# A DRAIN of its own on GpSimd, ahead of the last expert's four scatters

## The chip, the cores and the metric

The kernel runs on one core of one Trainium2 chip. The core has five engines that follow their own instruction queues: TensorE (PE), VectorE (DVE), ScalarE (ACT), GpSimd (POOL) and SyncE (SP); 16 DMA engines move data beside them. The metric is the device time of one execution in microseconds; lower is better. Three executions of the kernel before took 489.33, 487.57 and 484.19 us, median 487.57 us.

## What is computed

Banded attention with eight global columns, whose output rows are the tokens of a mixture-of-experts layer: 3072 tokens of 512 values, 8 experts, top 1, at most 768 tokens per expert. The reference, cut to its core:

```python
x = attention(q, k, v)                       # 4 x 8 heads x 768 x 64 -> (3072, 512)
expert_idx = np.argmax(x @ w_gate, axis=1)
gate_w = softmax(x @ w_gate)[np.arange(N), expert_idx]
# disp[e]: the rows of x that go to expert e, in order, up to the capacity
h = np.maximum(np.einsum('ecd,edf->ecf', disp, w1), 0.0)
y = np.einsum('ecf,efd->ecd', h, w2)
out[i] = gate_w[i] * y[expert_idx[i], pos[i]]     # for each token that was kept
```

## The kernel before

The program has three stages. The first is attention with the gate's logits and the routing: it leaves the rows of x in a DRAM tensor (`xrows`), and each token's expert and place in tables on the chip. The second is a loop over the eight experts (e = 0 to 7), each with four blocks of up to 128 tokens. The third, `overflow`, is skipped by one branch (L1279) where no expert has more than four blocks, as in the profiled execution.

For one expert GpSimd first fetches the four blocks of rows by indirect DMAs (`fetch_rows`, L519: 128 rows of `xrows`, named by a column of indices). TensorE turns them, multiplies by w1 in eight steps (`layer1`, L548) and by w2 (`layer2`, L1122 to L1124, and `beside`, L1135, for a few rows of the last block), with every factor split in a high and a low part. At the end of an expert `last()` (L1245) closes the four output blocks: `finish` (L1022) scales a block by the tokens' gates on ScalarE into the tile `ysb` (L1024; the fourth block has three additions on VectorE, L1028), and the `scatter` that it returns (L1031) has GpSimd send the 128 rows of `ysb` to their tokens' rows of the output by an indirect DMA (L1032). `out_scatters` lists all scatters so far; `apart` tells the scheduler that they write different rows. `last()` of expert e runs inside the first step of expert e + 1, and for e = 7 behind the loop (L1259).

GpSimd issues no other DMAs. Over the whole program it issues 32 gathers (L519) and 32 scatters (L1032), four of each per expert.

PE, ACT and DVE follow the order in which the code is written. GpSimd's queue in this stage is ordered by Tile's scheduler. In the built program GpSimd's queue around the last expert reads: the seventh expert's four scatters, six branches, the last expert's four scatters, a register load from `nblk` (L1237), the branch over `overflow` (L1279), two semaphore instructions, and the closing sequence, which has the line of the launch (L1367): DRAIN, barrier with the other four engines, DRAIN, a clearing of the semaphores, DRAIN, second barrier. A scatter's instruction waits for the block in `ysb`, and for the DMA that used the same one of eight semaphores before. SP waits at the end until every DMA has landed, then joins the barrier.

Of the kernel before, what the change touches and what calls it, by code (L numbers as in the profile page):

```python
# [120 lines left out]
def fused(ctx: ExitStack, tc, q, k, v, wg, w1, w2, out, dims, n_global, n_local, cap):  # L121
    nc = tc.nc
    B, H, S, D = dims
    DM, E = wg.shape
# [41 lines left out]
    NOSYNC = mybir.DependencyInfo(mybir.DependencyClass.NoSync, mybir.DependencyReason.SCHED_ONLY)  # L166
# [294 lines left out]
    def apart(w, others):  # L461
        for o in others:
            tc.declare_no_dep(w.ins, o.ins, reason="each token has a row of its own")
        others.append(w)
# [17 lines left out]
    def token_rows(t, e, lo, hi):  # L482

        ids, gates = filled.rearrange("p c (e a) -> p c e a", a=RB)[:, :, e, lo:hi].rearrange("p c e a -> c p e a")
        nc.vector.tensor_scalar(t.bitcast(I32)[:, :, :, 0], ids, float(N), None, op0=ALU.add)
        nc.vector.tensor_copy(t[:, :, :, 1], gates)
# [54 lines left out]
    def layer1(e, f, h_ps, xh, xl, s, parts=(0, 1)):  # L541
        w = wparts[e * (NF // FP) + f // FP][0]
        w1h, w1l = w["h"], w["l"]
        fs = slice(f % FP * P, (f % FP + 1) * P)
        for part in parts:
            n = 2 * KC * part
            for c, (ww, xx) in ((c, t) for c in range(KC) for t in (((w1h, xh), (w1l, xh)), ((w1h, xl),))[part]):
                nc.tensor.matmul(h_ps[:, s], ww[:, c, fs], xx[:, c, s], start=n == 0, stop=n == 3 * KC - 1)  # L548
                n += 1
# [451 lines left out]
    def gather(gi, rows=(), xhl=None):  # L1001

        xh, xl = xhl or [moe.tile([P, KC, T4], F32R, name=n) for n in ("xh", "xl")]
        rows = list(rows)

        def fetch():
            for a in range(len(rows), FIXED):
                xg, ld = fetch_rows(moe, "xg", FIXED + 1, gi(a))
                rows.append(xg)
            return ld  # L1010

        def turn(a, ps=None):
            ps = bankC([P, KC, P]) if ps is None else ps.rearrange("p (c t) -> p c t", c=KC)
            turn_rows(ps, rows[a])
            o = slice(a * P, (a + 1) * P)
            nc.scalar.copy(xh[:, :, o], ps)
            nc.vector.tensor_tensor(xl[:, :, o], ps, xh.bitcast(F32)[:, :, o], op=ALU.subtract)
        return xh, xl, turn, fetch

    out_scatters = []  # L1020

    def finish(e, a, rows, y):  # L1022
        ysb = moe.tile([P, DM], F32, name="ysb", bufs=FIXED)
        nc.scalar.activation(ysb, y, AF.Copy, scale=rows[:, 1:2])  # L1024
        if a == FIXED - 1:

            for n, o, m in ((1, 2 * GR, 2 * GR), (0, GR, GR), (0, 3 * GR, GR)):
                nc.vector.scalar_tensor_tensor(ysb[0:m], y[o:o + m], gates[0:m, e, n:n + 1], ysb[0:m],  # L1028
                                               op0=ALU.mult, op1=ALU.add)

        def scatter():  # L1031
            w = nc.gpsimd.indirect_dma_start(  # L1032
                out=out, out_offset=bass.IndirectOffsetOnAxis(ap=rows.bitcast(U32)[:, 0:1], axis=0),
                in_=ysb, in_offset=None, bounds_check=N - 1, oob_is_err=False)
            apart(w, out_scatters)
        return scatter


# [57 lines left out]
    def load_arm(e):  # L1096
        arms[e] = nc.values_load(arm[0:1, e:e + 1], engines=[PE], min_val=0, max_val=NV - 1)
# [6 lines left out]
    def widths(e):  # L1104

        def among(lo, hi):
            if hi - lo == 1:
                yield FINE * (lo + FIRST_ARM)
                return
            mid = (lo + hi) // 2  # L1110
            with tc.If(arms[e] > mid - 1) as more:
                yield from among(mid, hi)
            with more.Else():
                yield from among(lo, mid)
        yield from among(0, NV)

    def layer2(e, f, a, y, hh, hl):
        w = wparts[e * (NF // FP) + f // FP][1]
        w2h, w2l = w["h"], w["l"]
        t = slice(a * P, (a + 1) * P)  # L1120
        fi = f % FP
        nc.tensor.matmul(y, hh[:, t], w2h[:, fi], start=f == 0, stop=False)  # L1122
        nc.tensor.matmul(y, hh[:, t], w2l[:, fi], start=False, stop=False)  # L1123
        nc.tensor.matmul(y, hl[:, t], w2h[:, fi], start=False, stop=f == NF - 1)  # L1124

    def beside(e, fs, w, hs):

        y = y_ps[FIXED - 1]
        a, rows = w // P, -(-(w % P) // GR) * GR
        if rows in (GR, 2 * GR):  # L1130
            n = P // rows
            for f in fs:
                o = f % n * rows
                hr = hs[f][2]
                nc.tensor.matmul(y[o:o + rows], hr[:, (a - SURE) * P:(a - SURE) * P + rows],  # L1135
                                 wparts[e * (NF // FP) + f // FP][1]["r"][:, f % FP], start=f < n, stop=f >= NF - n)

    def whole(w):

        return range(SURE, w // P + (w % P > 2 * GR))  # L1140
# [7 lines left out]
    def fetch(step, after=()):  # L1148
        if step < STEPS and step not in wparts:
            pieces[step] = raw_weights(step, moe, "wr", 4, after, plain)  # L1150
# [40 lines left out]
    for e in range(E):  # L1191
        xh, xl = xs[0:2]
        hs = hs0 if e == 0 else {}

        def second(fs, a, e=e, hs=hs):
            for f in fs:
                layer2(e, f, a, y_ps[a], *hs[f][0:2])

        for f in range(NF):
            step = (e * NF + f) // FP  # L1200
            if f % FP == 0:
                fetch(step + SPLIT + 1)
                split = pieces.pop(step + SPLIT, [])
            if f == 1 and 0 < e < E - 1:
                xs = gather(lambda a, e=e: gi[:, e + 1, a:a + 1])
                xs[3]()
            if f == 2 and e == 0:
                load_arm(0)
            if f == 4 and e + 1 < E:
                load_arm(e + 1)  # L1210
            h = h_ps[f % 2]

            fs = (f - 2,) if f > 1 else ()
            for a in range(SURE):
                second([i for i in fs if e > 0 or i >= EARLY], a)
            part = slice(FIRST * P if e == 0 and f < EARLY else 0, T4)
            for w in widths(e) if e > 0 or f > 1 else ():
                for a in whole(w):
                    second(fs, a)
                if f == 5:  # L1220
                    beside(e, range(0, 4), w, hs)
                layer1(e, f, h, xh, xl, slice(part.start, w))
            if f == 3 and e == 0:
                tb = moe.tile([P, E, FIXED, 2], F32, name="tb", bufs=1)
                token_rows(tb, slice(0, E), 0, FIXED)
                nc.vector.tensor_scalar(gi, tb.bitcast(I32)[:, :, :, 0], N - 1, None, op0=ALU.min)
                xs = gather(lambda a, e=e: gi[:, e + 1, a:a + 1])
                xs[3]()
            hidden(hs, f, part)
            if f == 0 and last is not None:  # L1230
                last()
            if f == 3 and e == 0:
                to = take_beside(tb)
            if f == 5 and e == 1:
                count_blocks()
            if f == 4 and e == E - 1:
                most = nc.values_load(nblk[:, E:E + 1], min_val=0, max_val=max(RB, FIXED + 1))  # L1237
            for piece in () if f == 0 else split if f == 1 else split[2 * (f % FP):2 * (f % FP) + 2]:
                piece()

            turned = {5: (0, 1), 6: (2, 3)} if e == 0 else {3: (0,), 4: (1,), 5: (2,), 6: (3,)}
            for a in turned.get(f, ()) if e + 1 < E else ():
                xs[2](a)

        def last(e=e, second=second, hs=hs):  # L1245
            for a in range(SURE):
                second((NF - 2,), a)
            for w in widths(e):
                beside(e, range(4, NF), w, hs)
                for a in whole(w):  # L1250
                    second((NF - 2, NF - 1), a)
            rest = [finish(e, a, to[:, e, a - SURE], y_ps[a]) for a in range(SURE, FIXED)]
            rest[0]()
            for a in range(SURE):
                second((NF - 1,), a)
                finish(e, a, first["early"][:, a] if e == 0 and a < FIRST else tb[:, e, a], y_ps[a])()
            rest[1]()

    last()  # L1259
    manual[0].__exit__(None, None, None)  # L1260

# [109 lines left out]
```

## Time and profile before

| | |
|---|---|
| three executions | 489.33, 487.57, 484.19 us; median 487.57 us |
| the profiled execution, its own time | 488.32 us |
| its span, first to last instruction | 486.5 us |
| granted TensorE clock, mean | 0.969 of full speed |
| TensorE, matmuls | 452.5 us busy (93%) |
| VectorE, ScalarE | 287.4 us (59%), 282.5 us (58%) |
| GpSimd | 157.9 us (32%), 353 instructions |

Times in the profile are counted from the span's first instruction. Each engine has a sequencer, and rows of its instructions end in q (POOLq, SPq): DRAIN, semaphore and branch instructions are such rows. They are not counted as busy, and the chain of work that ended last, which the page follows back from the end, does not hold them all; it is followed from the last instruction that is counted as work. So what an engine does between its last work and the end of the span has to be asked for by line.

### The profile page before, as it was taken

To read this page: it belongs to the slowest core of one execution; us is meant where nothing else is said; L and a number is where in the kernel's file an instruction comes from. 1 tells how busy PE (TensorE), PEld (TensorE's weight loads), DVE (VectorE), ACT (ScalarE), POOL (GpSimd) and SP (SyncE) were. 2 spreads that over 40 slices of the span, in tenths; PEclk is the share of its full clock that TensorE was granted. 3 is DMA by queue.
4 is the path that set the end of the run, shared out by engine and by line. 5 is a ranking of instruction groups with operands and counts; after the bars stand their busy time and mean duration, and the time that the engine had idled before them with its cause. 6 is when DMAs were issued, how large, how long until landed. Compare 5 with 4: busy or idle time off the path is not lost.

```text
span 486.5 us, 11872 instructions
## 1 busy us (share of the span) xinstructions
PE 452.5 (93%) x4147; PEld 372.9 (77%) x4147; DVE 287.4 (59%) x935; ACT 282.5 (58%) x786; POOL 157.9 (32%) x353
## 2 busy tenths in 40 slices
PE   7999999989987699999999999999999999999690
PEld 3777877776776587888889989889889888887570
DVE  6687888778776626445646546456556455545421
ACT  5999898979862124445455555546556455446330
POOL 7117537789981104312103213103203203003002
PEclk9999999999996699999999999999999999999995
DMA  7988777787412078646536636446545545142001
GB/s 228 272 269 260 233 243 225 253 275 214 150 60 68 23 262 303 197 131 201 175 88 222 190 122 205 140 136 199 179 132 198 150 137 202 51 130 72 5 5 51
DMA packets 58701, 80.94 MB, mean 166 GB/s; under 512 B 6125, under 2 KB 34797, under 8 KB 58576
## 3 DMA queue, kind: packets, MB, share of 16 engines
q1 hardware_dynamic: 52912, 64.44, 42.0%
q0 software_dynamic: 5120, 14.69, 9.1%
q8 instruction: 94, 1.54, 1.3%
q14 instruction: 31, 0.25, 0.2%
q10 hardware_dynamic: 544, 0.02, 0.1%
HBM read 66.54 MB, written 14.68 MB: 167 GB/s over the span
## 4 chain that ended last, share of the span: by engine, by line
PE 51%; issue 28%; POOL 14%; DVE 3%; ACT 2%; POOLq 0%; DVEq 0%; ACTq 0%
PE bankC L548 17%; PE y L1122 5%; PE y L1124 5%; PE y L1123 5%; PE pair L689 3%; POOL put L449 3%; PE pair L723 3%; PE bankC L749 3%; PE bankC L752 3%; POOL out_dram L1032 2%; POOL own_row L444 2%; POOL xg L519 1%; PE bankC L500 1%; POOL w2l L267 1%; ACT sc L700 1%
## 5 line engine op out<-in xcount | busy, mean ns | idle before, releaser
L548 PE MATMUL bankC<-xh,w1h 128*128 128x416 f32 (+5 forms) x268 | 91.2, 345 | 2.6 <-issue 1.4
L1161 ACT ACTIVATE hh<-bankC 128x512 fp32r<-128x512 f32 (+1 forms) x67 | 38.7, 579 | 94.1 <-PE bankC L548 94.1
L548 PE MATMUL bankC<-xh,w1l 128*128 128x416 f32 (+5 forms) x268 | 89.8, 340 | 1.2 <-issue 1.2
L1162 DVE SCALAR_TENSOR_TENSOR hl<-bankC,hh 128x512 fp32r<-128x512 f32 (+1 forms) x67 | 44.6, 667 | 74.0 <-ACT hh L1161 73.6
L700 ACT ACTIVATE sc<-sc,mx 128x168 f32<-128x168 f32 (+1 forms) x192 | 80.3, 422 | 4.3 <-DVE mx L664 4.2
L1122 PE MATMUL y<-w2h,hh 128*128 128x512 f32 x192 | 79.8, 416 | 0.9 <-ACT hh L1161 0.8
L1124 PE MATMUL y<-w2h,hl 128*128 128x512 f32 x192 | 76.4, 398 | 0.0
L1123 PE MATMUL y<-w2l,hh 128*128 128x512 f32 x192 | 76.2, 397 | 0.0
L519 POOL DMA_INDIRECT xg<-xrows,gi x28 | 28.5, 1018 | 117.7 <-PE bankC L500 99.6
L548 PEld LDWEIGHTS bankC<-xh,w1h 128*128 128x128 f32 x268 | 51.6, 193 | 10.6 <-issue 6.0
L548 PE MATMUL bankC<-xl,w1h 128*128 128x416 f32 (+5 forms) x268 | 58.7, 341 | 0.6 <-issue 0.6
L664 DVE CUSTOM_DVE_ANT_0 sc<-pair,bias 128x168 f32<-128x168 f32 (+1 forms) x192 | 53.0, 317 | 9.7 <-PE pair L689 8.3
L1032 POOL DMA_INDIRECT out_dram<-ysb,to x16 | 15.9, 994 | 126.0 <-ACT ysb L1024 123.6
L548 PEld LDWEIGHTS bankC<-xh,w1l 128*128 128x128 f32 x268 | 51.7, 193 | 4.0 <-issue 1.3
L275 DVE TENSOR_TENSOR w1l<-wr,w1h 128x512 fp32r<-128x512 f32 x58 | 37.5, 689 | 27.8 <-ACT w1h L272 27.8
L1164 ACT ACTIVATE hr<-bankC 128x256 f32<-128x256 f32 x64 | 24.6, 385 | 49.3 <-DVE hl L1162 49.3
L275 DVE TENSOR_TENSOR w2l<-w2r,w2h 128x512 fp32r<-128x512 f32 x58 | 37.5, 688 | 19.2 <-ACT w2h L272 17.3
L548 PEld LDWEIGHTS bankC<-xl,w1h 128*128 128x128 f32 x268 | 47.9, 192 | 1.1 <-issue 0.4
L1122 PEld LDWEIGHTS y<-w2h,hh 128*128 128x128 f32 x192 | 36.6, 190 | 12.5 <-issue 4.6
L1124 PEld LDWEIGHTS y<-w2h,hl 128*128 128x128 f32 x192 | 36.4, 189 | 8.9
L1123 PEld LDWEIGHTS y<-w2l,hh 128*128 128x128 f32 x192 | 36.6, 191 | 6.1
L689 PE MATMUL pair<-K,q 64*64 64x168 f32 (+1 forms) x768 | 36.9, 309 | 1.3 <-DMA q<-in_q_dram 1.1
(190 smaller groups left out, 768.8 us busy)
## 6 DMA issues: line engine op xcount, KB each, us to landing
wr<-in_moe_w_dram SPq DMA_DIRECT2D x58, 256.0 KB
w2r<-in_moe_w_dram SPq DMA_DIRECT2D x58, 256.0 KB
K<-in_k_dram SPq DMA_DIRECT2D x24, 256.0 KB
q<-in_q_dram SPq DMA_DIRECT2D x24, 256.0 KB
v<-in_v_dram SPq DMA_DIRECT2D x24, 256.0 KB
xrows<-xr SPq DMA_DIRECT2D x23, 256.0 KB
v<-in_v_dram SPq DMA_DIRECT2D x20, 192.0 KB
wst<-in_moe_w_dram SPq DMA_DIRECT2D x12, 256.0 KB
```

The lines of the kernel that those rows point to most:

```text
L275: (nc.gpsimd if meanwhile else nc.vector).tensor_tensor(parts["l"][:, s], r, parts["h"].bitcast(F32)[:, s], op=ALU.subtract)
L519: ld = nc.gpsimd.indirect_dma_start(out=xg, out_offset=None, in_=xrows[0:n], in_offset=bass.IndirectOffsetOnAxis(ap=gi.bitcast(U32), axis= ...
L548: nc.tensor.matmul(h_ps[:, s], ww[:, c, fs], xx[:, c, s], start=n == 0, stop=n == 3 * KC - 1)
L664: x = nc.vector.tensor_tensor_reduce(out=un["sc"][:, a, 0:un["w"]], in0=un["ps"][hh][:, gg, :], in1=un["bias"][:, 4 * (u % 2) + a, :], sca ...
L689: made = nc.tensor.matmul(pss[hh][r * HP:(r + 1) * HP, gg, :], st_[i]["q"][rows, g, q0:q0 + HP], kq[rows, g, k0:k0 + w], start=True, stop= ...
L700: nc.scalar.activation(sc[:, a, 0:w], sc[:, a, 0:w], AF.Exp, bias=un["mx"][:, a:a + 1], scale=-1.0, accum_out=st_[i]["sm"][:, 4 * half + a ...
L1032: w = nc.gpsimd.indirect_dma_start(out=out, out_offset=bass.IndirectOffsetOnAxis(ap=rows.bitcast(U32)[:, 0:1], axis=0), in_=ysb, in_offset ...
L1122: nc.tensor.matmul(y, hh[:, t], w2h[:, fi], start=f == 0, stop=False)
L1123: nc.tensor.matmul(y, hh[:, t], w2l[:, fi], start=False, stop=False)
L1124: nc.tensor.matmul(y, hl[:, t], w2h[:, fi], start=False, stop=f == NF - 1)
L1161: nc.scalar.activation(hh[:, s], h[:, s], AF.Relu)
L1162: nc.vector.scalar_tensor_tensor(hl[:, s], h[:, s], 0.0, hh.bitcast(F32)[:, s], op0=ALU.max, op1=ALU.subtract)
```

## The change

One instruction is added to GpSimd's queue. In `last()` of the last expert (e = E - 1) `nc.gpsimd.drain()` is made, ordered behind every scatter made so far, that is those of experts 0 to 6, and ahead of the first scatter of the last expert. The orderings are of the kind NOSYNC: they fix places in GpSimd's own queue and add no semaphore. `scatter` returns its instruction, so that `last()` can name it. The whole diff:

```diff
@@ -1033,6 +1033,7 @@
                 out=out, out_offset=bass.IndirectOffsetOnAxis(ap=rows.bitcast(U32)[:, 0:1], axis=0),
                 in_=ysb, in_offset=None, bounds_check=N - 1, oob_is_err=False)
             apart(w, out_scatters)
+            return w
         return scatter
 
 
@@ -1250,7 +1251,13 @@
                 for a in whole(w):
                     second((NF - 2, NF - 1), a)
             rest = [finish(e, a, to[:, e, a - SURE], y_ps[a]) for a in range(SURE, FIXED)]
-            rest[0]()
+            if e == E - 1:
+                done = nc.gpsimd.drain()
+                for w in out_scatters:
+                    tc.add_manual_dep(done.ins, w.ins.name, NOSYNC)
+            w = rest[0]()
+            if e == E - 1:
+                tc.add_manual_dep(w.ins, done.ins.name, NOSYNC)
             for a in range(SURE):
                 second((NF - 1,), a)
                 finish(e, a, first["early"][:, a] if e == 0 and a < FIRST else tb[:, e, a], y_ps[a])()
```

In the built program the new DRAIN stands directly behind the seventh expert's fourth scatter, ahead of the six branches. It waits for no semaphore and sets none. Every other instruction of the five queues stands in the same order as before, with the same waits. Line numbers from 1036 on are one higher in the changed file and from 1253 on seven higher, so the DRAIN is at L1255 and the closing sequence has L1374.

## Rows read from the trace of the kernel before

**Rows 1.** Page, part 1: busy time, share of the span, instructions of each engine.

```profile
PE 452.5 (93%) x4147; PEld 372.9 (77%) x4147; DVE 287.4 (59%) x935; ACT 282.5 (58%) x786; POOL 157.9 (32%) x353
```

**Rows 2.** Chain that ended last, its last two pieces: start, length, what.

```profile
448.26 24.97 issue
...
477.31 0.98 POOL out_dram L1032
```

**Rows 3.** Closing line L1367, whole span: engine, operation, count, ns min/median/max, first to last start.

```profile
L1367 POOLq DRAIN  x3: 40/107/5306, 480.3 to 486.2; - x3
L1367 SPq DRAIN  x3: 7/7/13, 480.5 to 485.9; - x3
L1367 PEldq DRAIN  x2: 8/8/8, 475.4 to 486.0; - x2
L1367 ACTq DRAIN  x2: 8/8/8, 476.6 to 485.9; - x2
L1367 DVEq DRAIN  x2: 10/14/17, 478.9 to 485.9; - x2
```

**Rows 4.** Line L1367, GpSimd alone, 480.3 to 485.6 us.

```profile
L1367 POOLq DRAIN  x1: 5306/5306/5306, 480.3 to 480.3; - x1
```

**Rows 5.** Line L1367, 485.63 us to the end.

```profile
L1367 POOLq EVENT_SEMAPHORE  x4: 17/17/17, 485.7 to 486.3; - x4
L1367 SPq EVENT_SEMAPHORE  x2: 17/17/17, 485.8 to 486.4; - x2
L1367 POOLq DRAIN  x2: 40/74/107, 485.8 to 486.2; - x2
```

**Rows 6.** Stretches of the end: from:to, length, busy of each engine, TensorE clock, DMA share, GB/s.

```profile
448.26:473.46 25.20, 20.82 (x119) 16.07 (x118) 8.67 (x14) 9.93 (x21) 0.00 (x1) 1.00 0.03 7
473.46:478.29 4.83, 0.59 (x3) 0.15 (x1) 2.25 (x3) 1.46 (x3) 3.91 (x4) 0.80 0.33 111
478.29:480.32 2.03, 0.00 (x0) 0.00 (x0) 0.00 (x0) 0.00 (x0) 0.00 (x0) 0.50 0.12 38
480.32:485.63 5.31, 0.00 (x0) 0.00 (x0) 0.00 (x0) 0.00 (x0) 0.00 (x0) 0.50 0.00 2
485.63:486.50 0.87, 0.00 (x0) 0.00 (x0) 0.00 (x0) 0.00 (x0) 0.00 (x0) 0.50 0.00 0
```

**Rows 7.** Line L1367, SP's drains, 480.45 to 485.6 us.

```profile
L1367 SPq DRAIN  x2: 7/10/13, 480.5 to 480.6; - x2
```

**Rows 8.** Line L1358, the program's opening: GpSimd's drain there.

```profile
L1358 POOLq DRAIN  x1: 173/173/173, 0.4 to 0.4; - x1
```

**Rows 9.** GpSimd's DMAs: line, operation, names, count, busy us, mean ns, idle before.

```profile
L519 POOL DMA_INDIRECT xg<-xrows,gi x28 | 28.5, 1018 | 117.7 <-PE bankC L500 99.6 <-DVE gi L1226 16.3 <-issue 1.8
L1032 POOL DMA_INDIRECT out_dram<-ysb,to x16 | 15.9, 994 | 126.0 <-ACT ysb L1024 123.6 <-issue 1.8 <-DVE hl L1162 0.6
L1032 POOL DMA_INDIRECT out_dram<-ysb,tb x14 | 13.8, 984 | 4.3 <-issue 4.3
L519 POOL DMA_INDIRECT xge<-xrows,gie x2 | 2.3, 1165 | 0.8 <-POOL gie L494 0.5 <-issue 0.3
L519 POOL DMA_INDIRECT xg<-xrows,gif x2 | 2.1, 1051 | 20.0 <-DVE hl L1162 19.7 <-issue 0.3
L1032 POOL DMA_INDIRECT out_dram<-ysb,tbe x2 | 2.0, 984 | 0.6 <-issue 0.6
```

**Rows 10.** GpSimd in order of time, 443 us to the end: start, length, instruction, idle before.

```profile
445.99 0.98 POOL L1032 DMA_INDIRECT out_dram<-ysb,tb  x1 [0.30 <-issue]
447.28 0.98 POOL L1032 DMA_INDIRECT out_dram<-ysb,to  x1 [0.30 <-issue]
473.46 0.98 POOL L1032 DMA_INDIRECT out_dram<-ysb,to  x1 [25.20 <-ACT ysb L1024]
...
477.31 0.98 POOL L1032 DMA_INDIRECT out_dram<-ysb,to  x1 [0.31 <-issue]
```

**Rows 11.** All scatters to the output, whole span: time from issue to landing.

```profile
DMA to landing us min/median/max: 2.4/4.5/5.8
```

**Rows 12.** Branch over the overflow stage, line L1279, GpSimd's rows.

```profile
L1279 POOLq EVENT_SEMAPHORE  x2: 17/17/17, 480.1 to 480.2; - x2
...
L1279 POOLq COMPARE_BRANCH  x1: 53/53/53, 477.0 to 477.0; - x1
```

## The prediction, made before the changed kernel was timed

> **What bounds the kernel now, and what bounds its end.** I read the page's first part, then the chain, then what the chain leaves out. The first part shows TensorE at 93% of the span and GpSimd at 32% [rows 1], so over most of the span an instruction more on GpSimd cannot matter. The change sits near the end, so I cut the end into stretches [rows 6]. TensorE still computes until shortly after the last expert's first scatter: 20.82 us of matmuls in the 25.20 us before 473.46, 0.59 us behind it. Then come 4.83 us of scatters and 2.03 us with DMA traffic and no counted work. From 480.32 to 485.63 nothing is counted on any engine, the DMA share is 0.00, and 5.31 us go by. A last 0.87 us is barrier.
>
> The chain ends with the last scatter at 477.31 us, one of 0.98 us, and says nothing of the 8 us behind it [rows 2], because drains and barriers are not counted as work. Asked for by its line, the closing sequence shows them: GpSimd has three DRAINs there, of 40, 107 and 5306 ns [rows 3], and the long one starts at 480.3 [rows 4] and so fills the empty stretch exactly. The other engines' drains take 7 to 17 ns [rows 3]. SP has its two done at 480.6 [rows 7], and the barrier's semaphores follow at 485.7, at the moment GpSimd is out of its drain [rows 5]. So for 5.3 us the whole core waits for one DRAIN of GpSimd. That is on the path that sets the end, about 1.1% of the time.
>
> **Why it takes so long.** Four drains of GpSimd can be seen. The program's opening one took 173 ns [rows 8], with a few memsets and no DMA before it. The second and third of the closing sequence took 107 and 40 ns [rows 5], with no DMA between them and the drain before. Only the long one has DMAs behind it: 28 + 2 + 2 gathers and 16 + 14 + 2 scatters, 64 in all [rows 9]. And it did not wait for any of them to finish: the last scatter started at 477.31 [rows 10], scatters take 2.4 to 5.8 us to land [rows 11], traffic in its stretch is 2 GB/s at a share of 0.00 [rows 6], and SP, whose closing waits cover every landing, was through at 480.6 [rows 7]. So I take it for bookkeeping that GpSimd owes for each DMA it issued since its last drain, and put it at (5306 - 107) / 64 = 81 ns for each DMA, on a base of 107 ns. This split is an estimate; the trace has one long drain, and cannot show the slope.
>
> **The change, part by part.**
> - *Added: one DRAIN behind the seventh expert's fourth scatter.* That scatter is over at 447.28 + 0.98 = 448.26; the next instruction of GpSimd that works starts at 473.46, after 25.20 us of waiting for ScalarE [rows 10]. By the estimate the new drain takes 107 + 60 x 81 = 4.98 us. Queued behind it are six branches and the last expert's scatters. The branches are not recorded; one of the same kind stands between the third and fourth scatter of the seventh expert, where start to start is 447.28 - 445.99 = 1.29 us with a gap of 0.30, against a gap of 0.31 in the last expert, where no branch stands [rows 10]. So a branch costs 0 to 1.29 us, six at most 7.7. Should the drain also wait for the landing, 5.8 us after 447.28 at most [rows 11], GpSimd is ready at 453.1 + 5.0 + 7.7 = 465.8 at the latest, 7.7 us before it is needed. Cost on the path: nothing, covered by the wait for `ysb`. Nobody waits for GpSimd in that stretch, since the last gathers are long done. Without that cover it would cost its 5 us in full, and the change would do nothing.
> - *Shortened: the closing DRAIN.* Four DMAs are left to it: 107 + 4 x 81 = 0.43 us in place of 5.31, a gain of 4.87 us. With the 40 ns drain as base it is 0.37, with the 173 ns one 0.49. From below it is bounded by what is late next: SP's drains are through at 480.6 [rows 7], some 0.28 us after GpSimd begins its own at 480.32 [rows 6], so no more than 5.03 us can be had. From above it is bounded by the row itself, 5.31 us, a gain of nothing. I take 0.43, since three drains with nothing to account for are all short.
> - *The scatters themselves.* Whether they run differently behind a drain, no row shows. By group the 64 DMAs take 984 to 1165 ns on average, the program's first two gathers being the longest [rows 9]; if the first scatter behind a drain were like those, 0.18 us would be lost. I take zero: the first expert's scatters from `tbe` take 984 ns and the last expert's 0.98 us [rows 9, 10], so the number of DMAs behind an issue does not show in it. The branch at 477.0 and the 3.1 us to the next semaphore instruction at 480.1 [rows 12] stay.
>
> Sum: the profiled execution took 488.32 us, 1.8 more than its span of 486.5; with -4.87 it is 483.45 us. It ran 0.75 us above the median of the three runs, so against that median the forecast is 487.57 - 4.87 = **482.7 us**, a gain of 1.0%.
>
> **A rule against it.** The rows show a drain that starts more than 2 us after the last DMA instruction has ended and still takes 5.3 us. The Trainium skill ("PSUM — Partial Sum Buffer", section "Engine vs sequencer instructions") says that a drain waits for the engine to go fully idle. By that rule the length depends on what was issued last, the last four scatters are the same before and after, and the time would stay at 487.57 us. The skill's "VectorE: DVE Perf Modes" (section "The DRAIN you can't avoid") puts the drains of the opening and closing sequences at about 12 ns on all five engines; four engines agree here with 7 to 17 ns, GpSimd does not, and the measurement decides.
>
> **Rivals.**
> 1. *The long drain belongs to the last DMA, not to their number.* GpSimd would settle its queue once, at a fixed price, whenever at least one DMA was issued; or a drain would leave nothing settled, and the last would go through all 64 again. For it: one long drain fits a constant as well as a slope. Against it: the landings are over when it starts, and a constant of 5.3 us for a queue with nothing in flight has no counterpart in the trace. The new drain is covered, so the time is 487.57 us. Chance 0.08; the PSUM page's rule would come out here.
> 2. *Part of it is fixed.* If half of the 5.31 us is constant, the last drain takes 2.65 + 0.17 us and the time is 485.1. Chance 0.03.
> 3. *Slower: the new drain outlasts its cover.* Place: between 448.26 and 473.46. It decides from (25.20 - 7.7) / 60 = 0.29 us per DMA on if the branches are at their bound, 0.42 if they are free. The nearest row for work per DMA is 0.98 us for issuing one [rows 9]: 60 of them end at 507.1, the last scatters run 33.6 us late, and with the closing sequence unchanged the time is about 521. Against it: the closing drain settled 64 in 5.31 us. Chance 0.01, and 0.01 more for some loss over 1% that I don't see.
>
> That the drain is put elsewhere is not a case: in the built program it stands where the diff says, and all else stands as before.
>
> **How the numbers follow.** The forecast has 0.87. Over 1% against 487.57 is below 482.69, and about 1% is what measurement can tell from no change; the forecast of 482.7 lies on that bound, so half of its chance goes to each side: faster 0.45 (0.44 and a little from the others' spread), within 1% 0.53 (0.43 + 0.08 + 0.03 less that little), slower 0.02. The range: the forecast's own bounds are 4.81 to 5.03 us of gain, 482.5 to 482.8; the three runs lie 5.14 us apart, half of which is 2.6 on each side, so 479.9 to 485.4. I raise the upper end to 486.0, which takes in rival 2 and part of the spread of rival 1: **479.9 to 486.0**.
>
> **What would show it.** A DRAIN of about 5 us on GpSimd at the new line, starting near 448.3; the last expert's first scatter still released by ScalarE's `ysb`, with its gap of about 25 us unchanged; the longest DRAIN of the closing sequence at 0.37 to 0.49 us instead of 5306 ns; SP's barrier wait gone; the stretch from the last scatter's end to the end of the span 3.3 us instead of 8.2. If the closing drain stays at 5.3 us, rival 1 is right, whatever the median does. A new drain that is short while the closing one stays long would mean that neither waits for the count of DMAs. A first scatter later behind ScalarE than before is rival 3.

## The result, and the profile after

The changed kernel takes 481.76 us, median of 17 executions (478.5 to 486.44), against 487.41 us for the kernel before in 17 executions beside them. The ratio is 0.9895, with a 95% interval of 0.9865 to 0.9925, so the gain is 3.7 to 6.6 us of the 487.41, 5.1 us in the middle. The ratio leaves out the slow executions (492.03 us before, 486.44 us after), so it is not the quotient of the two medians. The profiled execution took 481.27 us, with a span of 479.4 us.

The closing sequence has line L1374 in the changed kernel, the added DRAIN L1255. These are GpSimd's rows of the two lines: operation, count, ns min/median/max, first to last start.

```profile
L1374 POOLq DRAIN  x3: 46/107/390, 478.2 to 479.1; - x3
...
L1255 POOLq DRAIN  x1: 7113/7113/7113, 443.7 to 443.7; - x1
```

The longest closing DRAIN took 5306 ns before [rows 3, 4] and takes 390 ns now: 4.92 us less. The row of the added one begins at 443.68, when GpSimd's sequencer reached it: the seventh expert's third scatter was still being issued, and the fourth started 1.16 us later. GpSimd in order of time (start, length, instruction, idle before):

```profile
444.84 0.98 POOL L1032 DMA_INDIRECT out_dram<-ysb,to  x1 [0.30 <-issue]
471.27 0.98 POOL L1032 DMA_INDIRECT out_dram<-ysb,to  x1 [25.45 <-ACT ysb L1024]
472.55 0.98 POOL L1032 DMA_INDIRECT out_dram<-ysb,tb  x1 [0.30 <-issue]
473.83 0.98 POOL L1032 DMA_INDIRECT out_dram<-ysb,tb  x1 [0.30 <-issue]
475.11 0.98 POOL L1032 DMA_INDIRECT out_dram<-ysb,to  x1 [0.30 <-issue]
```

The first of these rows is that fourth scatter. Its issue ends at 445.82 and the DRAIN at 443.68 + 7.11 = 450.79, so 4.97 us of the DRAIN lie behind the scatter. The wait for ScalarE's `ysb` runs on until 471.27, 25.45 us as against 25.20 [rows 10]: all of the 4.97 us are covered, with 20 us to spare. The last four scatters have their lengths and gaps of before. The end in stretches, cut as in [rows 6] (from:to, length, busy of PE, PEld, DVE, ACT, POOL, TensorE clock, DMA share, GB/s):

```profile
445.82:471.27 25.45, 20.83 (x119) 16.07 (x118) 8.67 (x14) 9.93 (x21) 0.00 (x1) 1.00 0.03 7
471.27:476.09 4.82, 0.59 (x3) 0.15 (x1) 2.25 (x3) 1.46 (x3) 3.91 (x4) 0.77 0.33 111
476.09:478.18 2.09, 0.00 (x0) 0.00 (x0) 0.00 (x0) 0.00 (x0) 0.00 (x0) 0.50 0.12 38
478.18:478.57 0.39, 0.00 (x0) 0.00 (x0) 0.00 (x0) 0.00 (x0) 0.00 (x0) 0.50 0.00 0
478.57:479.40 0.83, 0.00 (x0) 0.00 (x0) 0.00 (x0) 0.00 (x0) 0.00 (x0) 0.50 0.03 10
```

Only the fourth stretch differs, 0.39 us in place of 5.31. From the last scatter's issue to the end it is 3.3 us, where it was 8.2.

The two spans differ by more than that, 7.1 us. The other 2.2 us were there before the end began: the last expert's first scatter starts at 471.27 instead of 473.46. They are not the change's: the scatter right ahead of the added DRAIN was already 2.44 us earlier (444.84 against 447.28 [rows 10]), and the program's first scatter 2.19 us (214.50 against 216.69). The stretch from 140 to 222 us, where attention hands over to the experts, had TensorE at a mean granted clock of 0.88 of full speed (2.4 GHz) in the profile before and 0.96 after (first row before, second after; same columns):

```profile
140.00:222.00 82.00, 74.28 (x471) 62.58 (x470) 43.87 (x161) 30.52 (x71) 21.34 (x30) 0.88 0.51 165
```

```profile
140.00:222.00 82.00, 73.29 (x510) 61.97 (x505) 47.41 (x173) 33.66 (x81) 23.00 (x33) 0.96 0.51 169
```

An experiment below that has no added DRAIN (`e7_memsets`) reached that scatter at 471.45, and `e1_half`, which has one, at 472.85; so this start varies by 2 us and more from one profile to another, with or without the change. That the clock makes this difference is likely, but no run isolates it. A reader who set the two spans side by side would credit the DRAIN with 2 us too much.

### The profile page after: what moved, and what is told of

It is laid out like the page before. It is cut to its first block, busy times and chain, and to the rows that moved or that the text cites. A ratio compares the mean times of both kernels' runs of the same rounds, so it can differ in the third digit from the quotient of the medians.

```text
span 479.4 us, 11873 instructions
## 1 busy us (share of the span) xinstructions
PE 450.0 (94%) x4147; PEld 370.3 (77%) x4147; DVE 287.5 (60%) x935; ACT 282.4 (59%) x786; POOL 158.4 (33%) x353
## 4 chain that ended last, share of the span: by engine, by line
issue 57%; POOL 23%; PE 12%; DVE 6%; POOLq 1%; ACT 0%; DVEq 0%; ACTq 0%
POOL xg L519 6%; POOL out_dram L1032 4%; POOL put L449 4%; PE pair L689 3%; PE pair L723 2%; PE bankC L752 2%; POOL own_row L444 2%; PE bankC L749 2%; POOL w2l L267 2%; DVE sc L664 2%; POOL w1l L267 1%; PE pair L175 1%; PE pair L189 1%; POOL sm L704 1%; POOL w2h L272 1%
## 5 line engine op out<-in xcount | busy, mean ns | idle before, releaser
L689 PE MATMUL pair<-K,q 64*64 64x168 f32 (+1 forms) x768 | 38.1, 316 | 0.6 <-DMA q<-in_q_dram 0.4
```

Of the source, the lines that this page charges most:

```text
L689: made = nc.tensor.matmul(pss[hh][r * HP:(r + 1) * HP, gg, :], st_[i]["q"][rows, g, q0:q0 + HP], kq[rows, g, k0:k0 + w], start=True, stop= ...
```

## The experiments

The theory is that a DRAIN of GpSimd settles every DMA that GpSimd issued since its last DRAIN. Through the closing DRAINs with 4 and 64 DMAs goes a line of 62 ns plus 82 ns for each DMA. By it the added one, with 60, should take 4.98 us, and takes 4.97 from the end of the issue ahead of it. But three points on a line are few, and they also lie on a line over the time since the last DRAIN. So the experiments move the DRAIN, multiply it, uncover it, and add DMAs or other instructions.

**`e1_half`: the DRAIN four experts earlier.** The edit against the changed kernel, shortened; the second ordering has the same new condition:

```diff
-            if e == E - 1:
+            if e == 3:
                 done = nc.gpsimd.drain()
```

> The added DRAIN stands behind the third expert's scatters instead of the seventh's, so 33 of GpSimd's 64 DMAs are issued before it and 31 after it. Theory (a DRAIN settles each DMA issued since the last one, about 62 ns plus 82 ns for each, the line through 4, 60 and 64 DMAs): the added DRAIN lasts 2.77 us from the moment the scatter ahead of it is issued, the closing one 2.60 us, the two together 5.4 us. Rival (the cost grows with the time since the last DRAIN, which fits the same three points with 11 ns for each us): the added DRAIN comes near 335 us and lasts 3.7 us, the closing one comes 145 us later and lasts 1.7 us. Rival (fixed price whenever a DMA was issued): both 5.3 us.

```profile
L1255 POOLq DRAIN  x1: 6034/6034/6034, 293.3 to 293.3; - x1
...
L1374 POOLq DRAIN  x3: 46/107/2595, 479.9 to 483.1; - x3
```

The scatter ahead of the added one, in order of time:

```profile
294.52 0.98 POOL L1032 DMA_INDIRECT out_dram<-ysb,to  x1 [0.30 <-issue]
```

The closing DRAIN took 2595 ns, as the count of 31 says (2.60 us). The time since the last one, 181 us, would have made it 2 us, a fixed price 5.3; both fall. The added DRAIN missed: it came at 293 us, earlier than I had put it, and ended at 299.35, 3.85 us after the scatter ahead of it was issued (294.52 + 0.98), not 2.77. The one execution took 485.2 us.

**`e2_each`: a DRAIN ahead of every expert's scatters.** The edit against the changed kernel:

```diff
-            if e == E - 1:
-                done = nc.gpsimd.drain()
-                for w in out_scatters:
-                    tc.add_manual_dep(done.ins, w.ins.name, NOSYNC)
+            done = nc.gpsimd.drain()
+            for w in out_scatters:
+                tc.add_manual_dep(done.ins, w.ins.name, NOSYNC)
             w = rest[0]()
-            if e == E - 1:
-                tc.add_manual_dep(w.ins, done.ins.name, NOSYNC)
+            tc.add_manual_dep(w.ins, done.ins.name, NOSYNC)
```

> A DRAIN ahead of every expert's four scatters, so that each has only the DMAs since the one before to settle. Theory (count of DMAs): each of the middle ones lasts 0.4 to 0.8 us from the moment the scatter ahead of it is issued, all lie in GpSimd's waiting time, the closing one has 4 DMAs and lasts 0.39 us, and the time is that of the changed kernel, 481.8 us, ratio to before 0.99. Rival (a fixed price for a DRAIN that has DMAs behind it): each lasts some 5 us, and the ones ahead of gathers could delay them. Rival (a DRAIN waits until the DMAs have landed): each lasts 2.4 to 5.8 us, the landing time of a scatter.

All eight added DRAINs, the last of them alone, and the closing ones, by lines:

```profile
L1254 POOLq DRAIN  x8: 1149/4592/5604, 2.8 to 443.0; - x8
...
L1254 POOLq DRAIN  x1: 3833/3833/3833, 443.0 to 443.0; - x1
...
L1372 POOLq DRAIN  x3: 46/107/380, 476.9 to 478.2; - x3
```

The scatter that the last added one stands behind, in order of time:

```profile
444.14 0.98 POOL L1032 DMA_INDIRECT out_dram<-ysb,to  x1 [0.30 <-issue]
```

Only seven of the eight stand behind DMAs. The first expert's has no scatter ahead of it to be ordered behind, was put at the start of the program (2.8 us), among GpSimd's set-up, and is the one of 1149 ns. The closing DRAIN is short as expected, 380 ns. The middle ones are not: the last of them, with four DMAs, ended at 446.82, 1.70 us after the scatter was issued and 2.68 us after its start, and the scatters of the kernel before took 2.4 to 5.8 us to land [rows 11]. So the second rival, that a DRAIN also waits for the landing, has something to it, and the count alone fails while DMAs are on their way. The time is 482.37 us, ratio 0.9941 (0.9905 to 0.9977), faster than before and not to be told from the changed kernel, whose interval it meets between 0.9905 and 0.9925. More DRAINs bring nothing.

**`e3_late`: the same DRAIN behind the last expert's first scatter, without cover.** The edit against the kernel before, shortened; beside it `scatter` returns its instruction as in the change:

```diff
             rest[0]()
+            if e == E - 1:
+                done = nc.gpsimd.drain()
+                for w in out_scatters:
+                    tc.add_manual_dep(done.ins, w.ins.name, NOSYNC)
             for a in range(SURE):
                 second((NF - 1,), a)
-                finish(e, a, ...)()
+                w = finish(e, a, ...)()
+                if e == E - 1 and a == 0:
+                    tc.add_manual_dep(w.ins, done.ins.name, NOSYNC)
```

> The added DRAIN stands behind the last expert's first scatter instead of ahead of it, where nothing covers it: scatters two to four are queued behind it. Theory (count of DMAs, and the gain came from the cover): it has 61 DMAs and lasts 5.06 us, the second scatter starts some 5 us later behind the first than before, the closing DRAIN has 3 DMAs and lasts 0.31 us, and the two cancel: 487.4 us, ratio to before 1.00, 5 us slower than the changed kernel. Rival (the gain has nothing to do with the cover, a second DRAIN is what makes the closing one short): 482 us, ratio 0.99.

The added DRAIN and the closing ones, by lines:

```profile
L1256 POOLq DRAIN  x1: 6270/6270/6270, 469.6 to 469.6; - x1
...
L1374 POOLq DRAIN  x3: 46/107/627, 481.1 to 482.8; - x3
```

The last four scatters, in order of time:

```profile
469.87 0.98 POOL L1032 DMA_INDIRECT out_dram<-ysb,to  x1 [25.34 <-ACT ysb L1024]
476.78 0.98 POOL L1032 DMA_INDIRECT out_dram<-ysb,tb  x1 [5.92 <-issue]
478.06 0.98 POOL L1032 DMA_INDIRECT out_dram<-ysb,tb  x1 [0.31 <-issue]
479.34 0.98 POOL L1032 DMA_INDIRECT out_dram<-ysb,to  x1 [0.30 <-issue]
```

486.64 us, ratio 1.0018 (0.9987 to 1.0048): the gain is gone, and the interval lies apart from the changed kernel's. The DRAIN ended 5.06 us after the first scatter's issue, what 61 DMAs give, and the gap to the second scatter is 5.92 instead of 0.30. The closing DRAIN took 0.63 us instead of 0.31; it ended 2.41 us after the last scatter's start, and that scatter was still on its way when it began: the last packet of GpSimd's DMA queue ended at 481.26, the DRAIN began at 481.13. So it is not enough to have a DRAIN: it must lie where GpSimd has nothing to do.

**`e5_behind`: the changed kernel and one more DRAIN behind the last four scatters.** The edit against the changed kernel:

```diff
             rest[1]()
+            if e == E - 1:
+                done = nc.gpsimd.drain()
+                for w in out_scatters:
+                    tc.add_manual_dep(done.ins, w.ins.name, NOSYNC)
```

> The changed kernel with one more DRAIN directly behind the last expert's fourth scatter, ahead of the register load and the branch. It has 4 DMAs that are still on their way. Theory (count alone): it ends 0.39 us after the fourth scatter is issued, the closing DRAIN has none left and lasts 0.05 to 0.11 us, and the branch, which now comes behind it, is some 2.5 us later: 484 us, ratio to before 0.994. Rival (a DRAIN also waits for the landing): it ends no sooner than 2.4 us after that scatter's start, 1.4 us after its issue, and the time is 485 us or more.

The DRAIN behind the scatters and the first of the closing ones, by lines:

```profile
L1266 POOLq DRAIN  x1: 4765/4765/4765, 473.9 to 473.9; - x1
...
L1378 POOLq DRAIN  x1: 62/62/62, 482.0 to 482.0; - x1
```

The scatter ahead of it, in order of time:

```profile
475.02 0.98 POOL L1032 DMA_INDIRECT out_dram<-ysb,to  x1 [0.30 <-issue]
```

It ended at 478.63, 2.63 us after the scatter's issue and 3.61 us after its start, where four landed DMAs take 0.39. The rival is right: a DRAIN also waits until what is on its way has landed. The packets of GpSimd's DMA queue, which the trace keeps, bear this out: the last one ended at 477.83, 0.80 us before the DRAIN did. The seven DRAINs of `e2_each` that stand behind DMAs ended 1.70 to 3.42 us after the last issue, but only 0.78 to 1.24 us after the last packet, so their ends follow the data and not the issue. The closing one, with nothing left, took 62 ns, which is the base that the line through 4 and 64 gives. 485.69 us, ratio 0.9987 (0.9948 to 1.0026), not to be told from the kernel before: one more in the wrong place loses most of what the first brought.

**`e4_tiny`, `e6_rows`, `e7_memsets`: more DMAs, or more of anything.** Each is the kernel before with additions in the seventh expert's code, which Tile's scheduler issued earlier. Their whole times hold other delays from those additions (490.67, 501.04 and 486.31 us in one execution each, with 487.31 for the kernel before beside them); only the closing DRAIN is read.

```diff
+            if f == 2 and e == E - 2:          # e4_tiny
+                tiny = moe.tile([1, 16, E], F32, name="tiny", bufs=1)
+                for n in range(16):
+                    nc.gpsimd.dma_start(out=tiny[:, n], in_=wg[n:n + 1, :])
```

```diff
+            if f == 2 and e == E - 2:          # e6_rows
+                thin = moe.tile([P, 16, 8], F32, name="thin", bufs=1)
+                for n in range(16):
+                    nc.gpsimd.indirect_dma_start(
+                        out=thin[:, n], out_offset=None, in_=xrows.rearrange("n (a b) -> (n a) b", b=8),
+                        in_offset=bass.IndirectOffsetOnAxis(ap=gi[:, 0, 0:1].bitcast(U32), axis=0),
+                        bounds_check=N - 1, oob_is_err=False)
```

```diff
+            if f == 2 and e == E - 2:          # e7_memsets
+                dull = moe.tile([P, 64, 2], F32, name="dull", bufs=1)
+                for n in range(64):
+                    nc.gpsimd.memset(dull[:, n], 0.0)
```

> The kernel before, with 16 more DMAs on GpSimd that move 32 bytes each (one row of the gate's weights into a tile nobody reads). Theory (count of DMAs, whatever they move): the closing DRAIN settles 80 DMAs and lasts 62 + 80 x 82 = 6.62 us, 1.31 us more than the 5.31 of before. Rival (count of rows or descriptors: 64 x 128 rows before, 16 rows more here): 5.32 us. Rival (bytes moved): 5.31 us.

> The kernel before, with 16 more indirect gathers of 128 rows of 32 bytes each into a tile nobody reads. Theory (count of DMAs): closing DRAIN 6.62 us, as with 16 DMAs of one row. Rival (count of rows or descriptors, a quarter more): 6.62 us too, so it differs from the run with one row each. Rival (bytes, 65 KB more beside 16 MB): 5.33 us.

> The kernel before, with 64 more memsets of two columns on GpSimd and no more DMAs. Theory (count of DMAs): closing DRAIN unchanged, 5.31 us. Rival (count of GpSimd's instructions of any kind, 353 before and 417 here): 6.27 us.

GpSimd's closing DRAINs of the three, in this order:

```profile
L1371 POOLq DRAIN  x3: 46/109/6607, 481.3 to 488.5; - x3
```

```profile
L1374 POOLq DRAIN  x3: 40/107/6612, 491.7 to 498.8; - x3
```

```profile
L1371 POOLq DRAIN  x3: 40/107/5306, 478.3 to 484.2; - x3
```

With 16 DMAs of one row 6607 ns, with 16 gathers of 128 rows 6612 ns, with 64 memsets 5306 ns, to the nanosecond that of before. The price is for a DMA, the same for these two kinds, and 64 more instructions of another kind add nothing to it.

With all DMAs landed, the closing DRAINs give: 0 DMAs 62 ns, 4 DMAs 390 and 380, 31 DMAs 2595, 64 DMAs 5306 twice, 80 DMAs 6607 and 6612. The line 62 + 82 n (62, 390, 2604, 5310, 6622) holds all of them within 15 ns. The point at 0 is the first closing DRAIN of `e5_behind` alone; the second and third closing DRAINs, also with no DMA to settle, took 107 to 109 and 40 to 46 ns in all runs.

The time from the start of the last expert's first scatter to the end of the span leaves out what differed earlier, and shows what each placing brought: 13.0 us before, 8.1 in the changed kernel, 10.5 in `e1_half`, 8.6 in `e2_each`, 13.2 in `e3_late`, 11.9 in `e5_behind`, 14.4 in both runs with 16 more DMAs, and 13.0 with the memsets. So 60 DMAs fewer at the end are worth 4.9 us, 33 fewer 2.5, and 16 more cost 1.4, where the line gives 4.9, 2.7 and 1.3.

## Why the prediction was right

- **What bounds the end** was right: the one DRAIN of 5.3 us was on the path, and taking it away moved the end by its length. `e3_late` shows it without relying on a comparison of spans: the same DRAIN uncovered gives no gain.
- **The cost of each DMA** was right. The prediction divided by 64 on a base of 107 ns and got 81 ns; the base with nothing to settle is 62 ns (`e5_behind`) and the slope 82 ns. The 107 ns DRAIN of the closing sequence is not a base: it is 107 or 109 in every kernel, whatever stands before it, and what it does is not settled here.
- **The closing DRAIN** was forecast at 0.43 us (0.37 to 0.49) and took 0.39. The term of the sum was 4.87 us; the profile shows 4.92, the ratio 5.1 with an interval of 3.7 to 6.6. The range of 479.9 to 486.0 was set by the spread of the three executions more than by the DRAIN, so that the median fell into it says less than this row does.
- **The added DRAIN** was forecast at 4.98 us and took 4.97 from the end of the scatter ahead of it, covered as forecast. Its row starts at 443.68 and not behind that scatter, as the prediction's signs had it (near 448.3 where the scatter ends at 448.26), since the sequencer reaches the DRAIN ahead of the scatter's start. A wait for the landing, which the text allowed for, is real, but here it added nothing to the time of the 60 DMAs.
- **The scatters** ran as before, at 0.98 us and gaps of 0.30, as taken.
- **The rivals** fell: a fixed price (1) by 390 ns, half of it fixed (2) by the base of 62 ns, and an added DRAIN that outlasts its cover (3) by 20 us of spare time. Rival 1's second form, a DRAIN that leaves nothing settled, falls with them.
- **The two rules.** A drain that waits for the engine to go fully idle (the Trainium skill, "PSUM — Partial Sum Buffer", "Engine vs sequencer instructions") is not contradicted, but it is not the whole: on GpSimd the wait includes the landing of DMAs (4765 ns in `e5_behind`), and behind an engine with nothing left to land it still took 5306 ns. The time that was drawn from this rule, 487.57 us, did not come: 481.76. About 12 ns on all engines (the Trainium skill, "VectorE: DVE Perf Modes", "The DRAIN you can't avoid") holds here for the other four, at 7 to 17 ns [rows 3], and not for GpSimd.
- **The chances** put the forecast on the bound of 1%, and that is where the result lies: 0.9895, with an interval that holds both sides of it.

One expectation failed: the count alone for DRAINs that come right behind their scatters (`e1_half`, `e2_each`, `e5_behind`, and the closing one of `e3_late`). The runs show that such a DRAIN waits for the landing. They do not show how the two waits add up: behind the last packet of GpSimd's queue it ended 0.78 and 0.80 us later with four DMAs and 2.00 us later with 33 (`e1_half`), where the line gives 0.39 and 2.77 us for landed ones, and with the 60 of the changed kernel the line holds from the last issue. So part of the settling overlaps the landing; how is open.

## What to carry to other kernels

Where GpSimd issues many DMAs, look at the program's closing DRAIN: here it cost 82 ns for each of them, and no list of busy work shows it. Ask for the closing line of the queues, and compare the end of the last work with the end of the span. A DRAIN in a place where GpSimd waits anyway, as late as there is a wait longer than 82 ns times the DMAs before it, takes that off the end. Issue it in such a wait only: uncovered it cost as much as it saved (`e3_late`), and a second one behind the last scatters, where nothing covers the landing, took back 3.7 of the 4.9 us (`e5_behind`).

## What the runs showed of the hardware

- GpSimd's first closing DRAIN takes 62 ns plus 82 ns for each DMA that GpSimd issued since its last DRAIN, once all have landed: at 0, 4, 31, 64 and 80 DMAs within 15 ns, the same for 16 DMAs of one row and 16 of 128 rows.
- A DRAIN of GpSimd also waits for DMAs on their way: with four of them, 4765 ns from its start, 2.63 us of it behind the last issue and 0.80 us behind the last packet.
- Memsets leave it as it is: with 64 more, 5306 ns as before.
- Profiles of kernels that differ in one DRAIN reached the same scatter between 469.87 and 473.46 us; in the two that were compared, the granted clock between 140 and 222 us was 0.96 and 0.88.
